# One pool of eight PSUM banks and a written-out order for every engine in a fused attention and feed-forward kernel

## The chip, the cores and the metric

The kernel runs on one core of one Trainium2 chip. The metric is the device time of one execution in microseconds. The kernel before was run three times: 359.77, 360.51 and 360.58 us, median 360.51 us.

## What is computed

The inputs are q, k and v, each (8, 8, 576, 64) in float32 (batch, heads, positions, head dimension), a bias table of 32 buckets by 8 heads, and the weights w_in (512, 2048) and w_out (2048, 512).

```python
scores = scale * np.matmul(q, k.transpose(0, 1, 3, 2))
...
scores = scores + bias.transpose(2, 0, 1)[None, :, :, :]
...
attn = np.exp(scores)
attn = attn / (np.sum(attn, axis=-1, keepdims=True) + 1e-09)
return np.matmul(attn, v).astype(np.float32)
```

The attention's result, 4608 rows of 512, goes through a feed-forward layer with a squared ReLU:

```python
h = np.maximum(x @ w_in, 0.0)
return (h * h @ w_out).astype(np.float32)
```

## The kernel before, in words

**Attention.** The 64 heads are worked on as 32 pairs (`pair`, L931; p = 4 * batch + hp). A pair's keys lie on TensorE's rows 0 to 63 for one head and 64 to 127 for the other, so that two score matmuls with 64 rows each run side by side (`scores_of`, L806: 128 keys by 512 queries, L815). The scores have the keys on the partitions. 576 keys are four key tiles of 128 and 64 last keys; 576 queries are 512 and 64 last queries, which have small matmuls of their own (L822). The 64 last keys of both heads share one matmul of 128 rows (`last_keys`, L1012). ScalarE takes the exponential from PSUM: 128 x 1024 elements at once over the two heads' banks (L997), 128 x 576 for the last keys (L1022), 128 x 256 per head for the last queries (`exp_of_last`, L831). VectorE multiplies the result by the table of exp(bias) (L728). `values` (L751) multiplies by v with a column of ones (L754, L761), and VectorE divides by the sum (L775, L780). The first batch goes in halves (`half_of_pair`, L840).

**Feed-forward.** The 4608 rows are nine groups of 512 (`layers`, L1483). The first product (L1501, or L1451 in halves for the first group) leaves 128 x 512 in a bank; ReLU takes it to SBUF (L1530, in this kernel always on ScalarE as `RELU_DVE` is 0), and VectorE squares it (L1540). Some units are done with seven products in place of eight (`by_sevens`, L1378). The second product also takes seven products in place of eight (`second`, L1204), combined by VectorE (L1232) or ScalarE (L1238), and SyncE stores the result.

**PSUM.** The eight banks are six tiles: two pairs of neighbouring banks (`sets_ps`, names st0 and st1, ring `r_set`) and four single banks (`g_ps`, names f0 to f3, ring `r_g`). Scores take a pair for each key tile, and two singles for the last queries.

**What sets the order.** The kernel's source first lists all work as operations (`Plan.add`), each with the engines that may do it, what it depends on and the buffers it uses. `Plan.schedule` then goes through them in planned time: each engine takes the operation that can start first, ties by due time; `DUES` gives due times for some 600 operations by their number. A buffer is taken from its ring when its first user starts, the one that has been free longest first (`min(ring.free)`). The instructions are then emitted in the order of planned starts, and each engine runs its own in that order. The waits between engines are not written in the source: the framework finds them from what each instruction reads and writes, in the order of emission.

In `pair`, batches from the second on compute two key tiles in one operation:

```python
            run([0, 1])
            last_keys()
            run([2, 3], True)
```

where `True` adds the last queries' eight matmuls to the operation, and their two exponentials after it. All of one operation's matmuls are issued one after the other.

Of the kernel before, what the change touches and what calls it, by code (L numbers as in the profile page):

```python
# [21 lines left out]
SCALE = 1.0 / 8.0  # L22
# [12 lines left out]
RELU_DVE = 0  # L35
# [31 lines left out]
DUES = """  # L67
# [52 lines left out]
"""  # L120
# [5 lines left out]
class Ring:  # L126


    def __init__(self, n, in_order=False):
        self.free = [(0.0, i) for i in range(n)]  # L130
        self.in_order, self.made, self.taken = in_order, 0, 0
# [39 lines left out]
STAY = 0.0  # L171


class Plan:
# [16 lines left out]
    def schedule(self):  # L191
        engines = ("PE", "ACT", "DVE", "POOL", "SP", "DMA", "XB")
        now = {"PE": 600.0, "ACT": 740.0, "DVE": 820.0, "POOL": 1300.0, "SP": 740.0, "DMA": 0.0, "XB": 0.0}
        mode = None
        waiting = {e: [] for e in engines}
        for op in self.ops:
            op.wait = len(op.deps)
            for d in op.deps:
                d.users.append(op)
            if not op.wait:  # L200
                for e in op.engs:
                    waiting[e].append(op)
        done = []
        while len(done) < len(self.ops):
            best = None
            for e in engines:
                pick = None
                for op in waiting[e]:
                    at = max(now[e], op.ready, self._buf_time(op))
                    if at == float("inf"):  # L210
                        continue
                    due = op.due if op.due > -1e8 else op.ready - 1e9
                    if e == "PE" and op.mode != mode:
                        due += STAY
                    key = (max(at, now[e]), due, op.seq)
                    if pick is None or key < pick[0]:
                        pick = (key, op)
                if pick is None:
# [9 lines left out]
            for x in op.engs:  # L228
                waiting[x].remove(op)
# [1379 lines left out]
```

## Time and profile before

| | |
|---|---|
| median of three runs | 360.51 us |
| profiled execution: first to last instruction (span) | 358.7 us |
| PE (TensorE matmuls) busy | 346.4 us, 97% |
| DVE (VectorE) busy | 297.5 us, 83% |
| ACT (ScalarE) busy | 272.6 us, 76% |
| POOL (GpSimd) busy | 170.6 us, 48% |
| matmuls | 4290 |

The page gives the profiled execution's span and not a time of its own beyond it; the median of the runs stands 1.8 us above the span. PE's busy time counts a matmul from its start to the moment its result has left the array, so neighbours overlap; what one matmul keeps the next from starting is read from the start times. In the views, a line such as L1204 is a line of the kernel; "x16" is the number of instructions merged in a row; square brackets hold idle time before a row and what ended it.

### The profile page before, as it was taken

The page shows a single profiled execution, that of the slowest core. Times are in us where ns is not written, and L with a number is a line of the kernel's source. Part 1 is how long each engine was busy: PE and PEld are TensorE (multiplying, and loading weights), DVE is VectorE, ACT ScalarE, POOL GpSimd, SP SyncE. Part 2 cuts the span into 40 slices and gives each one's busy share as a digit, 9 for nine tenths or more (in the row PEclk, how much of TensorE's full clock was granted, in tenths as well). Part 3 has the DMA queues.
Part 4 walks back from the last instruction along what each step waited for, and adds up shares of the span by engine and source line. Part 5 has one row for each costly group of instructions (what it writes and reads, how often), then busy time and mean ns, then how long its engine had stood idle before and what let it go on. Part 6 is the DMA issues. An engine that isn't in the chain of part 4 may idle for free.

```text
span 358.7 us, 10742 instructions
## 1 busy us (share of the span) xinstructions
PE 346.4 (97%) x4290; PEld 262.0 (73%) x4290; DVE 297.5 (83%) x673; ACT 272.6 (76%) x435; POOL 170.6 (48%) x289
## 2 busy tenths in 40 slices
PE   3988999999999999999999999999999999999996
PEld 3666788775587558877788568755867887888885
DVE  4888999666996799768896899798988798899993
ACT  4898997589966988678976887689889833899830
POOL 8886679698995896158478456221000000000000
PEclk9999999999999999999999999999999999999999
DMA  9999999999999999799999999863410032010023
GB/s 172 151 147 198 193 150 154 190 156 192 175 130 165 223 158 112 119 163 198 84 134 164 186 126 133 150 121 72 61 44 15 18 97 68 27 63 33 23 66 117
DMA packets 162210, 44.37 MB, mean 124 GB/s; under 512 B 145520, under 2 KB 162160, under 8 KB 162160
## 3 DMA queue, kind: packets, MB, share of 16 engines
q0 software_dynamic: 74208, 14.53, 54.6%
q1 hardware_dynamic: 87696, 28.86, 44.3%
q8 instruction: 33, 0.54, 0.6%
q10 hardware_dynamic: 256, 0.30, 0.3%
q14 instruction: 17, 0.14, 0.1%
HBM read 36.94 MB, written 9.44 MB: 129 GB/s over the span
## 4 chain that ended last, share of the span: by engine, by line
PE 88%; DMA 7%; POOL 2%; ACT 1%; issue 1%; DVE 0%; POOLq 0%
PE f L1204 31%; PE f L1501 20%; PE f L761 10%; PE st L815 8%; PE f L1378 7%; DMA w_in_sb<-in_moe_w_in_dram 5%; PE f L1451 3%; PE st L1378 3%; PE f L754 3%; PE st L1012 2%; DMA ks<-in_k_dram 2%; POOL va L368 2%; PE f L822 1%; PE f L1078 1%; POOL ks L368 0%
## 5 line engine op out<-in xcount | busy, mean ns | idle before, releaser
L997 ACT ACTIVATE pt<-st 128x1024 f16<-128x1024 f32 x112 | 111.1, 1031 | 23.0 <-PE st L815 22.8
L1501 PE MATMUL f<-xt,w_in_sb 128*128 128x512 f16 (+4 forms) x416 | 77.2, 330 | 0.0
L728 DVE TENSOR_TENSOR pt<-pt,tb_sb 128x512 f16<-128x512 f16 (+3 forms) x108 | 61.9, 581 | 12.6 <-ACT pt L997 9.3
L368 POOL DMA_DIRECT2D ks<-in_k_dram x79 | 55.9, 719 | 15.1 <-DMA kt<-ks 10.4
L1204 PEld LDWEIGHTS <-g 128*128 128x128 f16 x576 | 55.1, 98 | 7.6 <-issue 0.8
L368 POOL DMA_DIRECT2D qs<-in_q_dram x79 | 55.5, 712 | 8.1 <-DMA qt<-qs 6.2
L1530 ACT ACTIVATE rt<-f 128x512 f16<-128x512 f32 x80 | 47.3, 608 | 14.1 <-PE f L1501 12.7
L1501 PEld LDWEIGHTS <-w_in_sb 128*128 128x128 f16 x416 | 37.1, 98 | 26.7 <-issue 2.5
L761 PE MATMUL f<-va,pt 128*128 128x65 f16 x1280 | 53.2, 193 | 0.3 <-DMA va<-in_v_dram 0.3
L761 PEld LDWEIGHTS <-pt 128*128 128x128 f16 x1280 | 49.8, 97 | 1.3 <-issue 0.5
L1204 PEld LDWEIGHTS <-s 128*128 128x128 f16 x432 | 41.1, 98 | 5.8 <-issue 0.8
L1232 DVE SCALAR_TENSOR_TENSOR y<-f,y 128x512 f32<-128x512 f32 (+1 forms) x48 | 31.8, 665 | 12.5 <-PE f L1204 11.7
L815 PE MATMUL st<-qt,kt 64*128 64x512 f16 (+1 forms) x288 | 40.4, 361 | 1.0 <-DVE qt L716 0.6
L1540 DVE TENSOR_TENSOR g<-rt 128x512 f16<-128x512 f16 x80 | 34.3, 433 | 6.2 <-ACT rt L1530 5.3
L1204 PE MATMUL f<-wt,g 128*128 128x256 f16 x288 | 35.6, 273 | 0.0
L754 PE MATMUL f<-vm,pm 128*128 128x130 f16 x160 | 35.5, 222 | 0.0
L1204 PE MATMUL f<-w_out_sb,s 128*128 128x256 f16 x288 | 35.3, 273 | 0.0
L1204 PE MATMUL f<-w_out_sb,g 128*128 128x256 f16 x288 | 34.7, 273 | 0.1
L780 DVE TENSOR_TENSOR x<-f,r 128x384 f16<-128x384 f32 (+1 forms) x64 | 30.9, 485 | 0.9
L645 POOL CAST va<-f 128x512 f16<-128x512 f32 x24 | 16.7, 702 | 30.8 <-DMA f<-in_v_dram 17.5
L974 POOL COPY kz<-kt 64x64 f16<-64x64 f16 x55 | 19.4, 354 | 20.2 <-DMA kt<-ks 17.1
L831 ACT ACTIVATE pt<-f 128x256 f16<-128x256 f32 x64 | 22.9, 404 | 5.9 <-PE f L822 4.5
(112 smaller groups left out, 532.4 us busy)
## 6 DMA issues: line engine op xcount, KB each, us to landing
out_dram<-y SPq DMA_DIRECT2D x34, 256.0 KB, 2.8
f<-in_v_dram SPq DMA_DIRECT2D x24, 256.0 KB, 4.9
ks<-in_k_dram POOLq DMA_DIRECT2D x48, 64.0 KB, 5.2
qs<-in_q_dram POOLq DMA_DIRECT2D x48, 64.0 KB, 4.4
w_in_sb<-in_moe_w_in_dram POOLq DMA_DIRECT2D x4, 512.0 KB, 10.7
w_out_sb<-in_moe_w_out_dram POOLq DMA_DIRECT2D x4, 512.0 KB, 8.9
ks<-in_k_dram POOLq DMA_DIRECT2D x7, 144.0 KB, 5.6
qs<-in_q_dram POOLq DMA_DIRECT2D x7, 144.0 KB, 5.5
```

What stands on the lines that cost most here:

```text
L368: lambda: io(eng.dma_start(out=out_(), in_=in_())),
L728: io(nc.vector.tensor_tensor(out=a, in0=a, in1=t, op=MULT))
L754: nc.tensor.matmul(ps[:, i, :, :], pm[:, c : c + 128], vm[:, hp, :, 0:65], start=True, stop=False)
L761: nc.tensor.matmul(ps[:, i, e, :], pt[:, (2 * jt + e) * S + c : (2 * jt + e) * S + c + 128], va[:, jt, 2 * hp + e, 0:65], start=False, sto ...
L815: nc.tensor.matmul(banks[i][:, e, :], kt[rw[e], ts(jt, 128)], qt[rw[e], ds(q0, n)], start=True, stop=True)
L997: nc.scalar.activation(out=p5(pts[pb.slot])[:, jt, :, 0:512], in_=sets_ps[st.slot], func=EXPF, scale=SCALE)
L1204: nc.tensor.matmul(home[bf.slot][:, ts(s_, HALF)], left(c, s_), right(c), start=(c == 0 and (s_ == 0 or apart) and (own or i not in before ...
L1232: nc.vector.scalar_tensor_tensor(out=dst, in0=ps, scalar=OSC, in1=ys[y[plus].slot][:, cs], op0=MULT, op1=mybir.AluOpType.add,)
L1378: nc.tensor.matmul(ps()[:, ds(HALF * f + a, z - a)], left()[:, kk, ts(f, 128)], right(a, z)[:, kk, :], start=(first_ and f == 0 and a == 0 ...
L1501: nc.tensor.matmul(g_ps[bank.slot][:, a:z], w_in_sb[:, kk, ts(nt, 128)], xt_sb[:, kk, c : c + z - a], start=(kk == 0), stop=(kk == 3),)
L1530: io(nc.scalar.activation(out=rts[rb.slot], in_=g_ps[bank.slot], func=RELUF))
L1540: nc.vector.tensor_tensor(out=gs[gb1.slot][:, nt, :], in0=rts[rb.slot], in1=rts[rb.slot], op=MULT)
```

## The change

1. `TURNS` replaces `DUES`: five lists (PE, ACT, DVE, POOL, SP) name every operation by its number in the order in which that engine does it, 2112 in all. The list also fixes the engine where there was a choice. `Plan.schedule` still works out planned starts, for the order of emission and for which buffer of a ring is taken; at each step it takes the engine whose next entry can start first.
2. All eight banks are one tile and one ring. A pair of banks is any two that the ring gives; the exponential reads them with a stride (`in_two`).
3. Scores are one operation per key tile, and the last queries one of their own with one exponential of 128 x 512 for both heads.
4. ReLU may be done by VectorE (`RELU_DVE` is 9), squares by ScalarE.

The operations of a pair are numbered anew: from the second batch on a pair has twelve (score and exponential of key tiles 0 and 1, of the last keys, of key tiles 2 and 3, of the last queries) in place of ten.

```diff
-RELU_DVE = 0
+RELU_DVE = 9
-DUES = """
...
+TURNS = {
+    "PE": """
...
+1006 936 1033 1057 1059 1055 1101 1053 1102 1038 1051 1222 1049 1104 1105 1112 1116 1065 1070 1121 1125 1218
+1220 1250 1130 1134 1216 1248 1141 1212 1252 1254 1145 1142 1138 1152 1160 1153 1244 1246 1214 1156 1109 1085
...
+    "ACT": """
...
+927 1185 906 937 938 1060 1056 1054 1058 1223 1050 1052 1106 1219 1221 1251 1217 1249 1255 1213 1139 1143 1253
...
-    def schedule(self):
+    def schedule(self, order):
...
+        queues = {e: [self.ops[i] for i in l] for e, l in order.items()}
+        for e, l in queues.items():
+            for op in l:
+                op.engs = {e: op.engs[e]}
...
+            for e, l in queues.items():
+                if heads[e] == len(l) or l[heads[e]].wait:
                     continue
-                if best is None or pick[0][0] < best[0][0]:
-                    best = (pick[0], e, pick[1])
+                op = l[heads[e]]
+                at = max(now[e], op.ready, self._buf_time(op))
+                if at < (float("inf") if best is None else best[0]):
+                    best = (at, e, op)
...
-    sets_ps = [psum.tile([128, 2, 512], FP32, name=f"st{i}") for i in range(2)]
-    g_ps = pv_ps = [psum.tile([128, 512], FP32, name=f"f{i}") for i in range(4)]
+    banks_ps = psum.tile([128, 8, 512], FP32, name="bank")
+    g_ps = pv_ps = [banks_ps[:, i, :] for i in range(8)]
...
-    r_set, r_g, r_lane = Ring(2), Ring(4), Ring(8)
+    r_g, r_lane = Ring(8), Ring(8)
...
+    def squared(o, out_, src):
+        if o.eng == "ACT":
+            io(nc.scalar.activation(out=out_, in_=src, func=SQUAREF))
+        else:
+            io(nc.vector.tensor_tensor(out=out_, in0=src, in1=src, op=MULT))
...
+    def in_two(st):
+
+        i, j = st[0].slot, st[1].slot
+        return banks_ps[:, i : j + 1 : j - i, :] if i < j else banks_ps[:, j : i + 1 : i - j, :]
...
+    def last_queries(qb, pb, deps, T, after):
+
+        lq = [Buf(r_g) for _ in range(2)]
+        o = P.add(
+            {"PE": 4 * mm(64)}, lambda: scores_of(qb.slot, [], [], 0, 0, [of_head(lq, e) for e in range(2)]), deps,
+            [qb, pb] + lq, T, after, "r",
+        )
...
-        def run(jts, last=False):
-            sets = [Buf(r_set) for _ in jts]
-            lq = [Buf(r_g) for _ in range(2)] if last else []
+        def run(jt):
+            st = [Buf(r_g) for _ in range(2)]
...
+            def ex():
+                io(
+                    nc.scalar.activation(
+                        out=p5(pts[pb.slot])[:, jt, :, 0:512], in_=in_two(st), func=EXPF, scale=SCALE,
                     )
-
-                exps[jt] = P.add({"ACT": act(1024)}, ex, [o], [st, pb], T)
-            if last:
-                exps["q"], exps["q1"] = exp_of_last(lq, pb, o, T)
+                )
+
+            exps[jt] = P.add({"ACT": act(1024)}, ex, [o], st + [pb], T)
...
-        if b < 1:
-            run([0])
-            run([1])
-            last_keys()
-            run([2])
-            run([3], True)
-        else:
-            run([0, 1])
-            last_keys()
-            run([2, 3], True)
+        run(0)
+        run(1)
+        last_keys()
+        run(2)
+        run(3)
+        exps["q"] = last_queries(qb, pb, evac, T, after)
...
-    for op in P.schedule():
+    for op in P.schedule({e: [int(i) for i in x.split()] for e, x in TURNS.items()}):
```

The same replacement of `r_set` by the one ring is made in `last_keys`, in the halves of the first batch, and in `by_sevens`; the squares of both kinds of first product go through `squared`.

More of the change, by code (lines that the diff above doesn't have):

```diff
@@ L63, in _bucket @@
     return np.where(n < half, n, large).astype(np.int64)
-DUES = """
[52 rows of a table removed]
-"""
+TURNS = {
+    "PE": """
[26 rows of a table added]
+""",
+    "ACT": """
[17 rows of a table added]
+""",
+    "DVE": """
[29 rows of a table added]
+""",
+    "POOL": """
[11 rows of a table added]
+""",
+    "SP": """
[8 rows of a table added]
+""",
+}
 class Ring:
     def __init__(self, n, in_order=False):
-        self.free = [(0.0, i) for i in range(n)]
+        self.n, self.free = n, [(0.0, i) for i in range(n)]
         self.in_order, self.made, self.taken = in_order, 0, 0
@@ L170, in over @@
     return 40.0 if e == "POOL" else 0.0
-STAY = 0.0
 class Plan:
@@ L189, in land @@
         return op
-    def schedule(self):
-        engines = ("PE", "ACT", "DVE", "POOL", "SP", "DMA", "XB")
+    def schedule(self, order):
         now = {"PE": 600.0, "ACT": 740.0, "DVE": 820.0, "POOL": 1300.0, "SP": 740.0, "DMA": 0.0, "XB": 0.0}
         mode = None
-        waiting = {e: [] for e in engines}
+        queues = {e: [self.ops[i] for i in l] for e, l in order.items()}
+        for e, l in queues.items():
+            for op in l:
+                op.engs = {e: op.engs[e]}
+        moves = {e: [] for e in ("DMA", "XB")}
         for op in self.ops:
@@ L199, in schedule @@
                 d.users.append(op)
[L200 to L203, printed above, removed]
+            if not op.wait and op.fn is None:
+                moves[next(iter(op.engs))].append(op)
+        done, heads = [], dict.fromkeys(queues, 0)
         while len(done) < len(self.ops):
             best = None
[L206 to L218, printed above, removed]
-                    continue
-                if best is None or pick[0][0] < best[0][0]:
-                    best = (pick[0], e, pick[1])
+            for e, l in queues.items():
+                if heads[e] == len(l) or l[heads[e]].wait:
+                    continue
+                op = l[heads[e]]
+                at = max(now[e], op.ready, self._buf_time(op))
+                if at < (float("inf") if best is None else best[0]):
+                    best = (at, e, op)
+            for e, l in moves.items():
+                for op in l:
+                    at = max(now[e], op.ready)
+                    key = (at, op.due if op.due > -1e8 else op.ready - 1e9, op.seq)
+                    if best is None or at < best[0] or (best[1] == e and key < best[3]):
+                        best = (at, e, op, key)
             assert best is not None, "the plan is stuck"
-            (at, _, _), e, op = best
+            at, e, op = best[:3]
             took = op.engs[e]
@@ L227, in schedule @@
                 mode = op.mode
-            for x in op.engs:
-                waiting[x].remove(op)
+            if e in queues:
+                heads[e] += 1
+            else:
+                moves[e].remove(op)
             op.eng, op.start, op.end = e, at, at + took
@@ L247, in schedule @@
                     )
-                    for x in u.engs:
-                        waiting[x].append(u)
+                    if u.fn is None:
+                        moves[next(iter(u.engs))].append(u)
             done.append(op)
@@ L805, in values, with of_head @@
         return o
+    def in_two(st):
+        i, j = st[0].slot, st[1].slot
+        return banks_ps[:, i : j + 1 : j - i, :] if i < j else banks_ps[:, j : i + 1 : i - j, :]
+    def of_head(st, e):
+        i, j = st[0].slot, st[1].slot
+        return g_ps[(min(i, j), max(i, j))[e]]
     def scores_of(slot, banks, jts, q0, n, lq):
@@ L815, in scores_of @@
                     nc.tensor.matmul(
-                        banks[i][:, e, :], kt[rw[e], ts(jt, 128)], qt[rw[e], ds(q0, n)], start=True, stop=True
+                        banks[i][e], kt[rw[e], ts(jt, 128)], qt[rw[e], ds(q0, n)], start=True, stop=True
                     )
@@ L825, in scores_of @@
                 )
-    def exp_of_last(lq, pb, o, T):
-        def ex(e):
+    def last_queries(qb, pb, deps, T, after):
[5 more added lines that the diff above has]
+        def ex():
             io(
                 nc.scalar.activation(
-                    out=p5(pts[pb.slot])[:, :, e, 512:S],
-                    in_=g_ps[lq[e].slot][:, 0:256].rearrange("p (j s) -> p j s", j=4),
-                    func=EXPF, scale=SCALE,
+                    out=p5(pts[pb.slot])[:, :, :, 512:S].rearrange("p j e s -> p e j s"),
+                    in_=in_two(lq)[:, :, 0:256].rearrange("p e (j s) -> p e j s", j=4), func=EXPF, scale=SCALE,
                 )
             )
-        return [P.add({"ACT": act(256)}, lambda e=e: ex(e), [o], [lq[e], pb], T) for e in range(2)]
+        return P.add({"ACT": act(512)}, ex, [o], lq + [pb], T)
     def half_of_pair(p, part, turned):
@@ L851, in scores @@
         def scores(jt, last=False):
-            st = Buf(r_set)
-            lq = [Buf(r_g) for _ in range(2)] if last else []
+            st = [Buf(r_g) for _ in range(2)]
             def score():
-                banks = [sets_ps[st.slot][:, :, ts(j, 256)] for j in range(2)]
-                scores_of(qb.slot, banks, [jt, jt + 1], q0, 256, [g_ps[x.slot] for x in lq])
-            took = 2 * mm(256) + 10 + (4 * mm(64) if last else 0)
-            o = P.add({"PE": took}, score, evac + ready, [st, qb, pb] + lq, T, 0.0, "r")
+                banks = [[of_head(st, e)[:, ts(j, 256)] for e in range(2)] for j in range(2)]
+                scores_of(qb.slot, banks, [jt, jt + 1], q0, 256, None)
+            o = P.add({"PE": 2 * mm(256) + 6}, score, evac + ready, st + [qb, pb], T, 0.0, "r")
             def ex():
@@ L908, in half_of_pair @@
                 (512, lambda: tt(view(pb, 4 * S + 256, two + [[1, 256]]), tab(hp, 128, 256, 1)), [exps[2]] + tabs_done[2:6]),
-                (640, lambda: tt(view(pb, 6 * S + 256, two + [[1, 320]]), tab(hp, 0, 320, 1)), [exps[2], exps["q"], exps["q1"]] + tabs_done[0:5]),
+                (640, lambda: tt(view(pb, 6 * S + 256, two + [[1, 320]]), tab(hp, 0, 320, 1)), [exps[2], exps["q"]] + tabs_done[0:5]),
                 (192, lambda: tt(p4s[pb.slot][:, 384:S], tm_sb[:, hp, :]), [exps["k"]] + tm_done),
@@ L980, in pair, with ex @@
         exps = {}
-        def run(jts, last=False):
-            sets = [Buf(r_set) for _ in jts]
-            lq = [Buf(r_g) for _ in range(2)] if last else []
+        def run(jt):
+            st = [Buf(r_g) for _ in range(2)]
             def score():
-                scores_of(qb.slot, [sets_ps[st.slot] for st in sets], jts, 0, 512, [g_ps[x.slot] for x in lq])
-            took = len(jts) * mm(512) + 10 + (4 * mm(64) if last else 0)
-            o = P.add({"PE": took}, score, evac, sets + [qb, pb] + lq, T, after, "r")
+                scores_of(qb.slot, [[of_head(st, e) for e in range(2)]], [jt], 0, 512, None)
+            o = P.add({"PE": mm(512) + 3}, score, evac, st + [qb, pb], T, after, "r")
             if p == 4 * B - 1:
                 last_scores.append(o)
-            for jt, st in zip(jts, sets):
-                def ex(jt=jt, st=st):
-                    io(
-                        nc.scalar.activation(
-                            out=p5(pts[pb.slot])[:, jt, :, 0:512], in_=sets_ps[st.slot], func=EXPF, scale=SCALE
-                        )
-                    )
-                exps[jt] = P.add({"ACT": act(1024)}, ex, [o], [st, pb], T)
-            if last:
-                exps["q"], exps["q1"] = exp_of_last(lq, pb, o, T)
+            def ex():
+                io(
+                    nc.scalar.activation(
+                        out=p5(pts[pb.slot])[:, jt, :, 0:512], in_=in_two(st), func=EXPF, scale=SCALE
+                    )
+                )
+            exps[jt] = P.add({"ACT": act(1024)}, ex, [o], st + [pb], T)
         def last_keys():
-            st = Buf(r_set)
+            st = [Buf(r_g) for _ in range(2)]
             def score():
@@ L1012, in score @@
                         nc.tensor.matmul(
-                            sets_ps[st.slot][:, half, 0:HQ], kzs[qb.slot], qts[qb.slot][:, ts(half, HQ)],
+                            of_head(st, half)[:, 0:HQ], kzs[qb.slot], qts[qb.slot][:, ts(half, HQ)],
                             start=True, stop=True,
@@ L1016, in score @@
                     )
-            o = P.add({"PE": 2 * mm(HQ)}, score, evac + spread, [st, qb, pb], T, after, "f")
+            o = P.add({"PE": 2 * mm(HQ)}, score, evac + spread, st + [qb, pb], T, after, "f")
             def ex():
@@ L1023, in ex @@
                         out=p4s[pb.slot][:, 0:S].rearrange("p (h s) -> p h s", h=2),
-                        in_=sets_ps[st.slot][:, :, 0:HQ], func=EXPF, scale=SCALE,
+                        in_=in_two(st)[:, :, 0:HQ], func=EXPF, scale=SCALE,
                     )
                 )
-            exps["k"] = P.add({"ACT": act(S)}, ex, [o], [st, pb], T)
-        if b < 1:
-            run([0])
-            run([1])
-            last_keys()
-            run([2])
-            run([3], True)
-        else:
-            run([0, 1])
-            last_keys()
-            run([2, 3], True)
+            exps["k"] = P.add({"ACT": act(S)}, ex, [o], st + [pb], T)
+        run(0)
[4 more added lines that the diff above has]
+        exps["q"] = last_queries(qb, pb, evac, T, after)
         bands = [
@@ L1342, in by_sevens @@
                 late["ops", u] = late_sums(512, s_, terms, l_win + before, due + 10.0 * u, room)
-            home = r_set if g >= LATE else r_g
-            banks = {"a": Buf(home), "b": Buf(r_g), "c": Buf(r_g), "d": Buf(home)}
+            banks = {x: Buf(r_g) for x in "abcd"}
             y = {"u": Buf(r_f if g >= LATE else r_u), "v": Buf(r_y)}
@@ L1365, in by_sevens @@
                 st = banks[bk]
-                if bk in "ad" and g >= LATE:
-                    ps = lambda st=st: sets_ps[st.slot][:, 0, :]
-                else:
-                    ps = lambda st=st: g_ps[st.slot]
+                ps = lambda st=st: g_ps[st.slot]
                 parts = cut if i in (1, 2, 3) else [(0, HALF)]
@@ L1466, in by_halves, with square @@
                 r = one_of({"ACT": act(512), "DVE": dve(512)}, relu, [o], [bank, rb], 0.0)
-                def square(u=u, h=h, rb=rb):
-                    src = rts[rb.slot].rearrange("p (j s) -> p j s", j=2)
-                    io(
-                        nc.vector.tensor_tensor(
-                            out=gs[gb1.slot][:, 2 * u : 2 * u + 2, ts(h, HALF)], in0=src, in1=src, op=MULT
-                        )
+                def square(o, u=u, h=h, rb=rb):
+                    squared(
+                        o, gs[gb1.slot][:, 2 * u : 2 * u + 2, ts(h, HALF)],
+                        rts[rb.slot].rearrange("p (j s) -> p j s", j=2),
                     )
-                o = P.add({"DVE": dve(512, 2.0)}, square, [r], [rb, gb1], due - 1e5)
+                o = one_of({"DVE": dve(512, 2.0), "ACT": act(512)}, square, [r], [rb, gb1], due - 1e5)
                 for j in range(2):
@@ L1536, in layers @@
                 squares[g][nt].append(
-                    P.add(
-                        {"DVE": dve(512, 2.0)},
-                        lambda rb=rb, nt=nt, gb1=gb1: io(
-                            nc.vector.tensor_tensor(
-                                out=gs[gb1.slot][:, nt, :], in0=rts[rb.slot], in1=rts[rb.slot], op=MULT
-                            )
-                        ),
+                    one_of(
+                        {"DVE": dve(512, 2.0), "ACT": act(512)},
+                        lambda o, rb=rb, nt=nt, gb1=gb1: squared(o, gs[gb1.slot][:, nt, :], rts[rb.slot]),
                         [r], [rb, gb1], due - 1e5,
@@ L1571 @@
     layers(NG)
-    for x in DUES.split():
-        i, due = x.split(":")
-        P.ops[int(i)].due = float(due)
-    for op in P.schedule():
+    for op in P.schedule({e: [int(i) for i in x.split()] for e, x in TURNS.items()}):
         if op.fn is not None:
```

6 lines of the change are left out of this document (4 added, 2 removed), and 140 rows, old and new, of tables (DUES, TURNS).

## The prediction

> **What bounds the kernel now.** I read the page's busy shares first, then the busy time by stretches, then the waits of TensorE (PE), and last the start times of single matmuls.
>
> ```profile
> span 358.7 us, 10742 instructions
> ...
> PE 346.4 (97%) x4290; PEld 262.0 (73%) x4290; DVE 297.5 (83%) x673; ACT 272.6 (76%) x435; POOL 170.6 (48%) x289
> ```
>
> ```profile
> core 0: us, PE busy (x) PEld busy (x) DVE busy (x) ACT busy (x) POOL busy (x), PEclk, DMA share, GB/s
> 0.00:36.00 36.00, 26.91 (x526) 20.50 (x526) 26.84 (x83) 28.65 (x47) 28.28 (x54) 1.00 1.31 167
> 36.00:300.00 264.00, 263.90 (x3276) 193.53 (x3274) 222.35 (x508) 206.73 (x324) 142.30 (x235) 1.00 1.14 134
> 300.00:339.00 39.00, 39.00 (x344) 33.43 (x342) 34.99 (x63) 32.64 (x58) 0.00 (x0) 1.00 0.09 30
> 339.00:359.00 20.00, 16.55 (x152) 14.58 (x150) 13.27 (x23) 4.59 (x8) 0.00 (x0) 0.99 0.28 93
> ```
>
> From 36 us on PE never stands still until its last matmul: 263.90 of 264.00 and 39.00 of 39.00 us, at a granted clock of 1.00. Idle time is left in the first 36 us (9.1 us) and in the last 3 us. A busy PE need not be a fast one, so I look at when matmuls start.
>
> ```profile
> 128.63 0.38 PE L1501 MATMUL f<-xt,w_in_sb 128*128 128x512 f16 x1
> 128.84 0.60 PE L1378 MATMUL f<-tx,w_in_sb 128*128 128x256 f16 x4
> 129.28 1.89 PE L1501 MATMUL f<-xt,w_in_sb 128*128 128x512 f16 x8
> ```
>
> Columns: start, length, engine, line, tiles, weights, result, count. After one matmul of 512 columns the next starts 0.21 us later, after four of 256 the next one 0.44 us later (0.11 each). So each column costs about 0.42 ns, and the listed 0.38 us is 0.17 us longer than what keeps the next matmul waiting: the result leaves the array that much later. There is one more cost between neighbours:
>
> ```profile
> 35.65 0.60 PE L1451 MATMUL f<-xt,w_in_sb 128*128 128x256 f16 x4
> 36.18 0.60 PE L815 MATMUL st<-qt,kt 64*128 64x512 f16 x4
> 36.62 0.28 PE L822 MATMUL f<-qt,kt 64*128 64x64 f16 x8
> 36.83 0.23 PE L754 MATMUL f<-vm,pm 128*128 128x130 f16 x1
> ```
>
> Four full-height matmuls of 256 columns should let the next start after 0.44 us; the 64-row one starts after 0.53. Four 64-row matmuls side by side two by two take 0.44 us, as they should, and the eight of 64 columns should take 0.11 us where the next full-height one starts after 0.21. Each change between full height and half height costs about 0.10 us (over all of them 0.096). The timeline of PE has 154 changes of height or width of the array (transposes of 96 x 64 among them), the first at 4.41 to 6.24 us and the last at 287.45 to 287.99 us:
>
> ```profile
> 4.41 0.56 PE L419 MATMUL f<-g,id_sb 32*128 32x8 f32 x2 [4.41 <-DMA id_sb<-c_id]
> 6.24 0.69 PE L947 MATMUL f<-id_sb,ks 96*64 96x96 f16 x12 [1.27 <-ACT ex_sb L424]
> ...
> 287.45 0.61 PE L815 MATMUL st<-qt,kt 64*128 64x512 f16 x4
> 287.99 0.82 PE L1501 MATMUL f<-xt,w_in_sb 128*128 128x384 f16 x4
> ```
>
> So the kernel is a chain of matmuls at their full rate, plus 154 x 0.096 = 14.8 us of changes, plus the first 36 us. The change alters none of the matmuls. It can win only changes and idle time at the start, and anything that makes PE wait between 36 and 339 us is lost in full.
>
> **The change part by part.**
>
> *Changes of height.* I numbered the operations in the order in which the source lists them (a pair from the second batch on has two more than before) and marked the scores of 64 rows and the transposes in PE's table. Its 599 entries change 133 times, against 154: scores of different pairs and the last queries stand two or three together (23 visits of two entries, 37 of three, 3 of one). 21 x 0.096 = 2.0 us less. The Trainium skill (TensorEngine Tiling (Array Packing), section Tiling Modes) says that every change of tiling mode drains TensorE, which speaks against cutting the scores up by key tile; the trace agrees that a change costs, and the table's count decides how many there are.
>
> *The first 36 us.* The order of loads and first matmuls is another one, but each engine has the same kinds of work, and PE's longest waits there are for things that the tables do not remove:
>
> ```profile
> PE f L419 <- DMA id_sb<-c_id: 4.4, 1, 4.4
> PE f L1451 <- DMA w_in_sb<-in_moe_w_in_dram: 1.3, 1, 1.3
> PE f L947 <- ACT ex_sb L424: 1.3, 1, 1.3
> ```
>
> The load of w_in is the 22nd entry of POOL's table, about where it is now. I take 0, and 2 us either way, which is more than the wait for w_in.
>
> *ScalarE and VectorE.* By the tables 35 more ReLUs go to VectorE and 44 squares to ScalarE, and 64 exponentials of 256 become 32 of 512.
>
> ```profile
> L1530 ACT ACTIVATE rt<-f 128x512 f16<-128x512 f32 x80 | 47.3, 608 | 14.1 <-PE f L1501 12.7 <-ACT pm L1022 0.9
> L831 ACT ACTIVATE pt<-f 128x256 f16<-128x256 f32 x64 | 22.9, 404 | 5.9 <-PE f L822 4.5 <-issue 1.2
> L1424 ACT ACTIVATE g<-rt 128x512 f16<-128x512 f16 x32 | 20.0, 630 | 0.9
> L1540 DVE TENSOR_TENSOR g<-rt 128x512 f16<-128x512 f16 x80 | 34.3, 433 | 6.2 <-ACT rt L1530 5.3
> L1464 DVE TENSOR_SCALAR rt<-f 128x512 f16<-128x512 f32 x1 | 0.7, 682 | 0.0
> ```
>
> ScalarE: -35 x 0.608 + 44 x 0.630 - 64 x 0.404 + 32 x 0.608 = 0.0 us. VectorE: +35 x 0.682 - 44 x 0.433 = +4.8 us, to 302. Both stay far under PE's 346, which covers them; if that cover went they would still be 56 us short of being the bound. I take 0.
>
> *The one tile of eight banks.* This is the term that decides. The waits between engines come from the framework, which compares accesses within a tile. An access that strides over banks of a tile counts for it as the whole stretch from the first bank to the last: an exponential that reads banks 1 and 6 counts as touching 1 to 6. This is a property of the software, not of the chip, and before's trace cannot show it, since there a pair is a tile of two neighbouring banks. In the new kernel two things follow. An exponential also waits for products that were emitted ahead of it into banks in between, and a product emitted behind it into such a bank waits until the exponential has ended.
>
> How often do the pairs stand apart? The ring gives the bank that has been free longest. Following that rule down the five tables with the durations written in the source (used for which bank comes, never for a time of the kernel), I get two banks for each of the 188 activations over a pair (112 exponentials of key tiles, 28 of last keys, 32 of last queries, 16 of the first batch): only 51 pairs are neighbours; 40 are two apart, 25 three, 34 four, 16 five, 18 six, 4 seven. An example from the quoted rows of the tables: PE has 1218 1220 1250 1130 1134 1216, with banks 1 and 6; 0 and 4; 2 and 7; 3; 3; 1 and 6. The exponentials 1219, 1221 and 1251 are emitted behind 1220, 1130 and 1134. So 1219 (1 to 6) waits for 1220 (bank 4), and 1250 (bank 2) waits for 1219; 1221 (0 to 4) waits for 1130 (bank 3) and 1134 for 1221; 1251 (2 to 7) waits for 1134, and 1216 for 1251. PE and ScalarE, side by side today, take turns.
>
> What does one turn cost?
>
> ```profile
> L997 ACT ACTIVATE pt<-st 128x1024 f16<-128x1024 f32 x112 | 111.1, 1031 | 23.0 <-PE st L815 22.8
> ```
>
> ```profile
> 173.97 0.02 issue
> 173.99 0.57 ACT rt L1530
> ...
> 178.01 0.04 issue
> 178.06 1.03 PE f L1204 x8
> ```
>
> The last matmul's result 0.17 us after the next could have started, 0.02 to ScalarE's start, 1.03 for the exponential, 0.05 to PE's next start: 1.27 us (0.90 for the last keys at 0.661, 0.85 for the last queries at 0.61). For each of the 188 I took the last product ahead of it and the first behind it in its stretch, and added up PE's work in between at the rates above. In 41 cases there is none, in 38 others less than the turn needs; together 61.8 us are missing, 59.0 if places that overlap are counted once. What stands in ScalarE's queue between product and exponential (0.61 for an eviction, 1.03 for another exponential) lengthens turns: runs of up to six ScalarE entries, each place counted once, give 77 us, of which 9 come out as well when each access holds only its own banks; before's 263.90 of 264.00 us say that such runs cost little, so I take 77 - 9 = 68. Queued behind a waiting product is all of PE; ScalarE and VectorE wait for what it does not deliver, which leaves them slack.
>
> The ends: 40 us if the banks fall a third better than I followed them, since the order of planned starts decides that; 105 us if besides each of the 28 later pairs' last exponential comes a full turn (1.03) late for `values` (28 x 1.03 = 29), on top of the 77. Nearest to the rows is 68.
>
> Sum against the profiled execution: 358.7 - 2.0 + 0 + 0 + 68 = 424.7 us. The median of the runs stands 1.8 us above the span, so 426.5 us; with the ends and 2 us for the start, 396 to 466.
>
> **The rivals.**
>
> *The stretches do not bind.* If a strided access holds only its two banks, or the pairs fall side by side, nothing of the 68 us comes. Counted that way, the same places miss 0.5 us in all in place of 61.8: the order is comfortable by its own banks. Then 360.5 - 2.0 = 358.5 us, 356.5 to 360.5 with the start: faster. For it speaks the saturated PE, against it the 137 pairs that stand apart. It decides if fewer than about 2 of 79 short places really wait (2.0 us / 0.78 us each). Chance 0.11.
>
> *Every key tile is a visit of its own.* If the entries that stand together in PE's table did not run together, 28 x 3 = 84 visits more at two changes each cost 84 x 2 x 0.096 = 16 us: 376.6 us. PE runs its list in order, so this needs a slip in my numbering. Chance 0.02.
>
> *The clock falls.* With PE stopping every few us, the granted clock could drop. In the first 36 us PE is busy 26.91 of 36.00 us and the clock stays 1.00; the new middle would be busy 264 of about 330, more than that. If a quarter of PE's 346 us ran at half the clock, 87 us come on top: 513 us. The Trainium skill (TensorE: Matmul & The Clock Gate, section on HAM oscillation) describes kernels in which PE stands idle so often between groups of matmuls that the clock swings; by that rule this kernel is a candidate, by the row above it is not. Chance 0.02.
>
> **How the numbers follow.** The forecast, turns between PE and ScalarE, has 0.85, of which 0.05 outside 396 to 466 us. That range holds 0.80; the likeliest value is 426.5. It is about 18% slower than before. A measurement of this kernel tells apart about 0.3%, 1.1 us. Faster by more: 0.08, from the first rival; within: 0.03, the rest of it where the start eats the 2 us; slower: 0.89.
>
> **What would show it.** Right: PE's busy share falls from 97% to some 82%, with idle time in the stretch from 36 us on; among PE's waits there are dozens for the exponentials (key tiles, last keys, last queries) of about a microsecond, and ScalarE's exponentials wait for products that are not scores, such as those of the feed-forward layer. The clock is 1.00. Changes of height number 133. Busy times of VectorE near 302 and ScalarE near 273. Wrong: a PE that is still busy 264 of 264 us, or whose waits are for evictions or for `values` and not for exponentials.

## The result, and the profile after

The changed kernel takes 438.34 us (median of four executions, 432.41 to 438.99) against 360.50 us before (359.77 to 360.58). The ratio is 1.207, 95% interval 1.198 to 1.216; it is formed from the two executions that lie within 1.5% of the fastest, while the median is over all four (438.34 / 360.50 = 1.216).

From the page of the changed kernel: the span, the busy shares, and the granted clock in 40 slices of the span.

```profile
span 437.2 us, 10676 instructions
...
PE 364.6 (83%) x4290; PEld 267.5 (61%) x4290; DVE 303.8 (69%) x670; ACT 279.4 (64%) x408; POOL 165.6 (38%) x289
...
PEclk9959999999999999989999999999999999999999
```

TensorE has the same 4290 matmuls and is busy 83% of the span instead of 97%. The same view by stretches as before (busy time of each engine, then clock, DMA share and GB/s):

```profile
0.00:36.00 36.00, 25.01 (x393) 18.40 (x394) 20.34 (x58) 21.43 (x31) 22.06 (x42) 0.81 0.97 129
36.00:379.00 343.00, 284.84 (x3405) 201.03 (x3405) 235.68 (x530) 220.20 (x312) 143.54 (x248) 1.00 0.83 106
379.00:418.00 39.00, 39.00 (x351) 34.18 (x350) 34.71 (x60) 33.72 (x60) 0.00 (x0) 1.00 0.13 42
```

In the middle TensorE now stands still for 58.2 of 343.00 us; before it was 0.1 of 264.00. The 39 us that follow are as full as they were. Two things are new at the start: 393 matmuls are done by 36 us instead of 526, and the clock there is 0.81. What the idle time waits for stands in the waits of PE (us in total, times, longest):

```profile
PE bank L1553 <- ACT pt L1061: 9.7, 12, 1.1
PE bank L1262 <- ACT pt L1061: 9.5, 8, 1.6
PE bank L879 <- ACT pt L1061: 7.8, 8, 1.4
PE bank L1074 <- ACT pt L1061: 5.6, 6, 1.1
PE bank L809 <- ACT pt L1061: 5.3, 5, 1.6
PE bank L1432 <- ACT pt L1061: 3.7, 5, 1.1
```

L1061 is the exponential of a key tile. Added up over all rows of this kind, PE waits for exponentials of scores 68 times, 57.5 us. Before, there is one such wait:

```profile
PE st L815 <- ACT pt L864: 0.3, 1, 0.3
```

L1553, L1262 and L1432 are products of the feed-forward layer; they need no exponential's result. In the waits of all engines, exponentials in turn wait for such products, and VectorE waits for exponentials:

```profile
DVE y L1290 <- ACT pt L1061: 15.3, 2, 10.2
DVE rt L1584 <- ACT pt L1061: 11.9, 6, 3.4
ACT pt L1061 <- PE bank L1262: 10.3, 10, 1.5
ACT pt L1061 <- PE bank L1553: 7.3, 9, 1.4
ACT pt L1061 <- DVE y L1290: 5.5, 1, 5.5
```

The prediction's worked example can be found in the timeline of PE (start, length, operation; idle time before a row and its releaser in brackets):

```profile
134.55 0.60 PE L879 MATMUL bank<-qt,kt 64*128 64x512 f16 x4
136.52 0.39 PE L879 MATMUL bank<-qt,kt 64*128 64x512 f16 x2 [1.36 <-ACT pt L1061]
136.84 1.05 PE L1262 MATMUL bank<-wt,g 128*128 128x256 f16 x8
139.00 1.03 PE L1262 MATMUL bank<-wt,g 128*128 128x256 f16 x8 [1.11 <-ACT pt L1061]
139.87 0.29 PE L1074 MATMUL bank<-qt,kz 128*128 128x288 f16 x1
141.21 0.53 PE L1074 MATMUL bank<-qt,kz 128*128 128x288 f16 x3 [1.05 <-ACT pt L1061]
141.57 1.04 PE L1262 MATMUL bank<-w_out_sb,s 128*128 128x256 f16 x8
143.89 0.61 PE L879 MATMUL bank<-qt,kt 64*128 64x512 f16 x4 [1.28 <-ACT pm L1084]
```

and in that of ScalarE:

```profile
135.44 1.02 ACT L1061 ACTIVATE pt<-bank 128x1024 f16<-128x1024 f32 x1 [5.53 <-DVE y L1290]
137.93 1.02 ACT L1061 ACTIVATE pt<-bank 128x1024 f16<-128x1024 f32 x1 [1.46 <-PE bank L1262]
140.13 1.02 ACT L1061 ACTIVATE pt<-bank 128x1024 f16<-128x1024 f32 x1 [1.18 <-PE bank L1262]
142.65 1.19 ACT L1084 ACTIVATE pm<-bank 128x576 f16<-128x576 f32 x2 [1.49 <-PE bank L1262]
```

Read the two together. The products 1130 and 1134 (the two L1262 rows with `wt,g`) go to bank 3 and have nothing to do with scores. Yet the exponential at 137.93 starts when 1130 has ended, 1134 starts at 139.00 when that exponential has ended, the next exponential at 140.13 when 1134 has ended, and the rest of 1216 at 141.21 when that one has. PE and ScalarE take turns. The first exponential of the row adds something that the prediction did not have: its releaser is a VectorE read (L1290). The scores were there at 135.15 (134.55 + 0.60), so of the 5.53 us in the bracket the read made only the last 0.3.

### The profile page after: what moved, and what is told of

Read it like the earlier page. It is cut to its first block, busy times and chain, and to the rows that moved or that the text cites. A ratio compares the mean times of both kernels' runs of the same rounds, so it can differ in the third digit from the quotient of the medians.

```text
span 437.2 us, 10676 instructions
## 1 busy us (share of the span) xinstructions
PE 364.6 (83%) x4290; PEld 267.5 (61%) x4290; DVE 303.8 (69%) x670; ACT 279.4 (64%) x408; POOL 165.6 (38%) x289
## 4 chain that ended last, share of the span: by engine, by line
PE 66%; ACT 21%; DVE 6%; issue 3%; POOL 2%; DMA 2%; ACTq 0%; DVEq 0%; POOLq 0%
PE bank L1262 22%; ACT pt L1061 14%; PE bank L1553 13%; PE bank L1432 8%; PE bank L816 7%; PE bank L879 6%; PE bank L1505 3%; PE bank L809 2%; ACT pm L1084 2%; ACT pt L901 2%; DMA va<-in_v_dram 2%; PE bank L1074 2%; ACT pt L931 1%; DVE pt L783 1%; POOL va L417 1%
## 5 line engine op out<-in xcount | busy, mean ns | idle before, releaser
L1061 ACT ACTIVATE pt<-bank 128x1024 f16<-128x1024 f32 x112 | 111.5, 1022 | 51.8 <-PE bank L879 12.7
L1553 PE MATMUL bank<-xt,w_in_sb 128*128 128x512 f16 (+4 forms) x416 | 79.4, 330 | 10.7 <-ACT pt L1061 9.7
L1262 PEld LDWEIGHTS <-g 128*128 128x128 f16 x576 | 54.9, 98 | 22.1 <-issue 13.9
L1553 PEld LDWEIGHTS <-w_in_sb 128*128 128x128 f16 x416 | 36.9, 97 | 41.2 <-issue 19.1
L879 PE MATMUL bank<-qt,kt 64*128 64x512 f16 (+1 forms) x288 | 45.0, 377 | 14.4 <-ACT pt L1061 7.8
L816 PE MATMUL bank<-va,pt 128*128 128x65 f16 x1280 | 54.7, 194 | 0.6 <-DVE pt L783 0.5
L1290 DVE SCALAR_TENSOR_TENSOR y<-bank,y 128x512 f32<-128x512 f32 (+1 forms) x48 | 31.6, 663 | 31.2 <-ACT pt L1061 15.3
L1262 PEld LDWEIGHTS <-s 128*128 128x128 f16 x432 | 41.2, 98 | 10.7 <-issue 5.9
L809 PE MATMUL bank<-vm,pm 128*128 128x130 f16 x160 | 35.7, 223 | 7.5 <-ACT pt L1061 5.3
L1262 PE MATMUL bank<-wt,g 128*128 128x256 f16 x288 | 36.7, 277 | 5.9 <-ACT pt L1061 3.8
L1262 PE MATMUL bank<-w_out_sb,g 128*128 128x256 f16 x288 | 35.9, 273 | 4.3 <-ACT pt L1061 3.9
L1262 PE MATMUL bank<-w_out_sb,s 128*128 128x256 f16 x288 | 36.9, 274 | 2.6 <-ACT pt L1061 1.1
L835 DVE TENSOR_TENSOR x<-bank,r 128x384 f16<-128x384 f32 (+1 forms) x64 | 30.8, 485 | 9.2 <-ACT pt L1061 4.9
```

Source lines behind the costliest of these rows:

```text
L809: nc.tensor.matmul(ps[:, i, :, :], pm[:, c : c + 128], vm[:, hp, :, 0:65], start=True, stop=False)
L816: nc.tensor.matmul(ps[:, i, e, :], pt[:, (2 * jt + e) * S + c : (2 * jt + e) * S + c + 128], va[:, jt, 2 * hp + e, 0:65], start=False, sto ...
L835: nc.vector.tensor_tensor(out=xs[xb.slot][:, qt0 : qt0 + nq, :].rearrange("p t (e d) -> p t e d", e=2), in0=ps[:, :, :, 0:64], in1=rs[rb.s ...
L879: nc.tensor.matmul(banks[i][e], kt[rw[e], ts(jt, 128)], qt[rw[e], ds(q0, n)], start=True, stop=True)
L1061: nc.scalar.activation(out=p5(pts[pb.slot])[:, jt, :, 0:512], in_=in_two(st), func=EXPF, scale=SCALE)
L1262: nc.tensor.matmul(home[bf.slot][:, ts(s_, HALF)], left(c, s_), right(c), start=(c == 0 and (s_ == 0 or apart) and (own or i not in before ...
```

## The experiments

I state three theories. **Stretches:** the added waits come only from the stretch that a strided access counts for. **Order:** the new order, or finer operations, makes PE and ScalarE take turns with any banks. **One tile:** a single tile of eight banks costs something in itself, strided or not.

**Only the banks renamed.** The order, the operations, the shapes and the one tile stay. After the schedule has been made, each buffer gets its bank from a table, chosen so that no pair's stretch holds a bank that is in use beside it; most pairs become neighbours by it.

```diff
+BANKS = """
+1077610325414072306765672371422324560160152367601323454457016722353401064010235424074564651467572356
...
-    for op in P.schedule({e: [int(i) for i in x.split()] for e, x in TURNS.items()}):
+    order = P.schedule({e: [int(i) for i in x.split()] for e, x in TURNS.items()})
+    names = iter("".join(BANKS.split()))
+    named = set()
+    for op in P.ops:
+        for x in op.bufs:
+            if x.ring is r_g and id(x) not in named:
+                named.add(id(x))
+                x.slot = int(next(names))
+    for op in order:
```

> Tables, order of emission, instructions and their number are those of the changed kernel; only the bank numbers are given anew, so that no exponential's stretch holds a bank that is written or read beside it. Theory (waits through the stretch): the 78 us that PE stands longer go, 356 to 361 us, PE busy 97%, 133 changes of height (2 us less than before). Rival (the order of the tables, the smaller score operations or one ring cost the time by themselves): 430 us or more, as with the old numbers.

Measured: 359.85 us against 360.37 us for the kernel before on the same chip, ratio 0.9989 (0.9967 to 1.0011). The whole slowdown is gone. The timeline of PE for the same operations in this kernel:

```profile
106.83 0.82 PE L890 MATMUL bank<-qt,kt 64*128 64x512 f16 x6
107.58 1.92 PE L1273 MATMUL bank<-wt,g 128*128 128x256 f16 x16
109.34 0.65 PE L1085 MATMUL bank<-qt,kz 128*128 128x288 f16 x4
109.83 1.04 PE L1273 MATMUL bank<-w_out_sb,s 128*128 128x256 f16 x8
110.80 0.61 PE L890 MATMUL bank<-qt,kt 64*128 64x512 f16 x4
```

and ScalarE beside it:

```profile
107.29 2.85 ACT L1072 ACTIVATE pt<-bank 128x1024 f16<-128x1024 f32 x3 [4.48 <-PE bank L890]
```

From the first row to the last it is 3.97 us instead of 9.34; the three exponentials run one after the other while PE goes on. Since both kernels issue the same matmuls in the same order, their spans can be cut at the same matmul, number 393 and some 3400 later, where the last 59 us begin. First the changed kernel, then the one with renamed banks:

```profile
0.00:36.14 36.14, 25.01 (x393) 18.40 (x394) 20.35 (x59) 21.52 (x31) 22.20 (x42) 0.81 0.97 129
36.14:378.14 342.00, 283.98 (x3401) 200.64 (x3401) 235.22 (x529) 220.11 (x311) 143.40 (x248) 1.00 0.83 106
```

```profile
0.00:26.63 26.63, 19.95 (x393) 15.49 (x394) 19.32 (x57) 20.32 (x31) 19.69 (x36) 1.00 1.22 159
26.63:298.10 271.47, 270.62 (x3403) 197.95 (x3401) 233.43 (x529) 214.15 (x313) 151.85 (x254) 1.00 1.12 135
```

So of the 80.0 us between these two profiled executions 9.5 lie ahead of the 394th matmul, 70.5 in the some 3400 that follow, and none behind them. Order is ruled out as the cause, and so is One tile. That an exponential over distant banks is slow in itself is ruled out too: one of a key tile takes 1022 ns on average in the changed kernel and 1027 in this one.

**Two exponentials, each within one bank.** Banks and order of the changed kernel; every exponential over a pair becomes two instructions without a stride over banks (shown for key tiles; the other three kinds likewise).

```diff
-                io(
-                    nc.scalar.activation(
-                        out=p5(pts[pb.slot])[:, jt, :, 0:512], in_=in_two(st), func=EXPF, scale=SCALE
-                    )
-                )
+                for x in range(2):
+                    io(
+                        nc.scalar.activation(
+                            out=p5(pts[pb.slot])[:, jt, x, 0:512],
+                            in_=of_head(st, x), func=EXPF, scale=SCALE,
+                        )
+                    )
```

> Banks and order of the changed kernel; each exponential over two banks is two instructions, one for each bank, so that none strides. Theory: waits through the stretch go though the banks stay apart; ScalarE pays 156 x (2 x 0.608 - 1.03) = 29 us and some more for the last keys and queries, to about 312 us, under PE: 358 to 368 us. Rival (order or far banks as such): 430 us or more.

Measured: 361.44 us, ratio 1.0031 (1.0008 to 1.0053). The banks are as far apart as in the changed kernel, and PE is busy 347.2 us, 97% of the span, again. ScalarE has 188 instructions more and is busy 281.6 us, 9.4 us more than with renamed banks; my forecast of about 312 us was too high.

**Two exponentials, each over both banks.** The control: again two instructions, but each takes half the columns of both banks.

```diff
-                            out=p5(pts[pb.slot])[:, jt, x, 0:512],
-                            in_=of_head(st, x), func=EXPF, scale=SCALE,
+                            out=p5(pts[pb.slot])[:, jt, :, ts(x, 256)],
+                            in_=in_two(st)[:, :, ts(x, 256)], func=EXPF, scale=SCALE,
```

> As the kernel of one bank per instruction in the number of instructions, but each of the two still strides over both banks and takes half of the columns. Theory: the stretch stays, so the waits stay, 436 to 455 us. Rival (two short instructions in place of one long are what helps): as fast as the kernel of one bank per instruction.

Measured: 446.29 us, ratio 1.236 (1.230 to 1.242). With the same number of instructions as the run above, the stride alone makes 85 us. The first of PE's waits are those of the changed kernel again:

```profile
PE bank L1558 <- ACT pt L1064: 10.3, 11, 1.2
PE bank L1267 <- ACT pt L1064: 10.3, 9, 1.7
PE bank L879 <- ACT pt L1064: 8.3, 8, 1.4
```

**The kernel before, with one tile.** Its own order; the banks become one tile, pairs remain neighbours.

```diff
-    sets_ps = [psum.tile([128, 2, 512], FP32, name=f"st{i}") for i in range(2)]
-    g_ps = pv_ps = [psum.tile([128, 512], FP32, name=f"f{i}") for i in range(4)]
+    banks_ps = psum.tile([128, 8, 512], FP32, name="bank")
+    sets_ps = [banks_ps[:, 0:2, :], banks_ps[:, 2:4, :]]
+    g_ps = pv_ps = [banks_ps[:, i, :] for i in (4, 5, 6, 7)]
```

> The kernel before with all banks in one tile, its pairs still neighbours (0 and 1, 2 and 3). Theory (only the banks in between wait): no stretch holds another's bank, 360.4 us. Rival (one tile for all banks costs by itself): towards the 437.7 us that the same order took with pairs three banks apart.

Measured: 360.35 us against 359.79, ratio 1.0030 (0.9998 to 1.0062). One tile by itself costs at most 0.6%, and perhaps nothing.

**The kernel before, with its pairs apart.** The same one tile (`banks_ps`), with the two pairs as banks 0 and 3, and 4 and 7; the four single banks lie inside these stretches.

```diff
+    sets_ps = [banks_ps[:, 0:4:3, :], banks_ps[:, 4:8:3, :]]
+    g_ps = pv_ps = [banks_ps[:, i, :] for i in (1, 2, 5, 6)]
```

> The kernel before, its own order and its own due times; only the banks are one tile, the two pairs are banks 0 and 3 and 4 and 7, the singles 1, 2, 5, 6. Theory: 156 exponentials over a stretch with two singles in it, at 0.3 to 0.5 us each as worked out for such distances: 400 to 435 us, PE waiting for exponentials. Rival (the tables' order is what costs): 360.5 us, as nothing of the order is touched.

Measured: 437.73 us, ratio 1.215 (1.209 to 1.220), just above the interval that I gave. None of the change's order is in this kernel, and it is as slow as the changed one. Three rows of its waits: PE, VectorE and ScalarE, each waiting for work that it has no data from.

```profile
PE bank L1205 <- ACT pt L998: 17.9, 20, 1.2
DVE r L776 <- ACT pt L998: 21.1, 17, 2.3
ACT pt L998 <- PE bank L1205: 22.7, 16, 3.7
```

**How much by products, how much by reads.** The run before made VectorE's waits as large as PE's, and the prediction had counted only products. Three kernels rename the banks of the changed kernel as the first run does, with other tables. In two of them stretches hold banks that PE writes and none that VectorE or ScalarE reads, by the planned times. Counted as in the prediction, 37.0 and 99.2 us are missing (the changed kernel: 59.0). The third has hardly any such products (1.3 us) but stretches over banks that are being read out.

> As the one with 99 us, but with banks drawn at random and no readers in a stretch: 55 of 188 places short, 37.7 us missing, 37.0 with overlapping places once. If the time goes with that count: 359.9 + 37 = 397 us, up to 410 with ScalarE's queue. If instead a few stretches of the program bring all of the loss: near 360 or near 438.

Measured: 402.64 us, ratio 1.120 (1.116 to 1.124).

> Tables and order of the changed kernel, banks renamed so that stretches hold as many banks as possible in which PE writes beside the exponential, and none that VectorE reads beside it. The prediction's count: 123 of 188 places short of PE's work, 105.0 us missing, 99.2 with overlapping places once. Theory that the count is right in size: 359.9 + 99 = 459 us, up to 480 with ScalarE's queue. If VectorE's reads were a large part of what the changed kernel lost, less than that share: near 430.

Measured: 475.61 us, ratio 1.319 (1.311 to 1.326). One of its four executions took 685.25 us, at a mean granted clock of 0.55; the ratio leaves it out, and no run shows what made the clock fall so far. In the profiled execution, at a mean of 0.975, the clock fell in the middle as well:

```profile
290.00:310.00 20.00, 14.09 (x165) 10.06 (x162) 10.17 (x22) 8.00 (x11) 9.38 (x17) 0.74 0.68 77
```

> The other way round: stretches hold banks that VectorE reads beside the exponential (78 places in planned time, against 73 in the changed kernel) and hardly any that PE writes (10 places short, 1.3 us missing, against 79 and 59 us). Theory that only products count, as in the prediction: 360 to 362 us. Theory that readers wait for the stretch too, and give their banks back late: 365 to 385 us, VectorE waiting for exponentials in front of evictions.

Measured: 377.87 us, ratio 1.051 (1.048 to 1.054); that only products count, 360 to 362 us, is ruled out. The waits of this kernel show both directions, VectorE behind an exponential and an exponential behind VectorE:

```profile
DVE y L1301 <- ACT pt L1072: 7.2, 5, 2.5
...
ACT pm L1095 <- DVE x L846: 4.0, 1, 4.0
ACT pt L1072 <- DVE rt L1595: 3.4, 6, 1.2
...
DVE r L841 <- ACT pt L1072: 2.9, 4, 1.1
```

Added up over the rows of VectorE's reads of banks, they wait for exponentials of scores 31 times, 24.6 us, against once, 3.0 us, in the renamed kernel.

Above the renamed kernel's 359.85 us, products alone cost 42.8 us for 37.0 counted and 115.8 for 99.2: 1.16 and 1.17 us for each us of the prediction's count (the larger one at a mean clock of 0.975, which is in its figure). The renamed kernel was timed on another chip, on which the kernel before took 360.37 us and not 359.79; by ratios to these the rates come to 1.18 and 1.16. The kernel with reads costs 18.0 us, of which 1.3 are products by the count; PE itself still waits 13 times, 6.4 us, for exponentials there, so not all of it need be waits of reads. These reads only share a stretch with the exponential, and neither side writes what the other reads; the rows show them ordered all the same.

## Why the prediction was right, point by point

**The cause is shown.** Waits through the stretch make the slowdown: renaming banks takes it away (359.85), dropping the stride takes it away (361.44) while the same number of strided instructions keeps it (446.29), and a stretch over busy banks brings it to the kernel before (437.73).

**Its size: right, and some microseconds short.** The prediction had 68 us for products and the queue of ScalarE. By the rate of the two product kernels, the 59.0 us counted come to 59.0 x 1.16 = 68.5 us: the runs put 16% on top of the bare count where the prediction had put 15% for ScalarE's queue. That the two agree so well is partly luck, since the 15% was a difference of two counts (77 - 9) and no run separates the queue from the rest. The median of the changed kernel lies 438.34 - 359.85 = 78.5 us above the renamed one, which leaves 10 us that the sum did not have.

**Two things were left out: reads and the clock.** The prediction considered what PE writes into a stretch, and not what VectorE and ScalarE read from it. The kernel with reads, at 78 such places by its count, lost 18.0 us; the changed kernel has 73. The prediction also held the clock at 1.00. The one execution of the changed kernel at a clock of 0.996, which is also that of the kernel with 37.0 us counted, took 432.41 us; there 432.41 - 359.85 - 68.5 = 4.1 us are left for the reads. In the other three the clock was 0.98, and they took about 6 us more. How much the reads make beyond that cannot be separated: reads and products meet in the same places.

**The first 36 us: taken as 0, with 2 us either way.** For the order of loads and first matmuls alone, this was about right: in the renamed kernel PE is idle 6.7 us in the first 36, against 9.1 before, 2.4 us less. The changed kernel's first 393 matmuls come 9.5 us later than the renamed one's all the same. Stretches in the first batch are not new there, as its 16 exponentials were among the 188 counted; PE is idle 11.1 us ahead of that point instead of 6.7. The rest is that the same matmuls keep PE busy 25.01 us instead of 19.95, while the clock fell to half:

```profile
18.00:19.00 1.00, 0.61 (x11) 0.40 (x9) 0.99 (x3) 0.90 (x1) 0.96 (x3) 1.00 1.19 158
19.00:20.00 1.00, 0.27 (x1) 0.10 (x1) 0.32 (x2) 0.92 (x3) 1.00 (x3) 1.00 1.61 169
20.00:21.00 1.00, 0.44 (x13) 0.44 (x13) 0.46 (x3) 1.00 (x3) 0.47 (x1) 1.00 1.28 190
21.00:22.00 1.00, 1.00 (x24) 0.73 (x22) 0.97 (x5) 0.70 (x1) 0.00 (x0) 0.65 1.24 199
22.00:33.00 11.00, 9.17 (x99) 6.14 (x98) 6.00 (x18) 5.99 (x10) 1.48 (x4) 0.50 0.52 84
```

These are pieces of the changed kernel's span; PE is busy 1.32 us of the three from 18 to 21 us, and from 22 to 33 us it has half the clock. What sets the fall off is not shown: in its first 4 us PE was busy only 0.56 us, and the clock was 1.00 from there to 21 us. "The clock is 1.00" was therefore wrong at the start and right in the middle (1.00 from 36 us on).

**Of the rivals,** the first (stretches do not bind, 358.5 us) is refuted, and so is a separate visit for every key tile: PE's trace has 134 changes of height or width, the table's 133 and the one behind the first two matmuls of 32 rows. The 154 of before include that one, so 20 changes are saved and not 21, 1.9 us and not 2.0. The third, the clock, came true in small. Executions of the changed kernel at a mean clock of 0.98 took 437.73 to 438.99 us and one at 0.996 took 432.41: some 6 us, not 87. The Trainium skill (TensorE: Matmul & The Clock Gate, section A second HAM failure mode: psum-queue depth-cycling) describes a kernel whose clock swings because PE is idle briefly, but often, between groups of matmuls. In the changed kernel the trace bears this out only at the start: the middle, with PE idle 58.2 of 343.00 us in pieces of about a microsecond, kept 1.00. With still more waits it did not, as the kernel with 99.2 us counted shows (0.74 from 290 to 310 us, and 685.25 us in the execution at 0.55).

**The 2.0 us from fewer changes** did not show as a gain. The renamed kernel has the fewer changes and hardly any of the turns, and is faster by 0.4 us, with an interval from 1.2 faster to 0.4 slower, so a net gain of 2.0 us lies outside it. Its middle gives some of the gain back: PE idles 0.85 of 271.47 us there, where before it idled 0.10 of 264.00. PE's busy time, 346.2 us against 346.4, does not show the 2.0 us either, and why is open.

**ScalarE and VectorE** carry what was worked out: 272.2 and 301.6 us in the renamed kernel, against 273 and 302. In the changed one they show 279.4 and 303.8 and idle time throughout.

## What to carry to other kernels

The number of a PSUM bank is part of the schedule: where one instruction strides over banks of a tile, every bank between them is ordered with it, for those who write and those who read, so pairs must be neighbours, or in a tile of their own, or be read by an instruction for each bank. A pool with free pairing can keep its order and still be cured, by giving out the bank numbers after the order is fixed. In a trace, such waits show where an engine that used to be saturated is released by an instruction that has no data for it.

## What the runs showed of the hardware that was not expected

- Half the clock for more than 11 us after three microseconds in which PE was busy 1.32 us, while PE idle for a sixth of the 343 us in the middle kept all of it; and a mean clock of 0.55 over a whole execution of 685.25 us in the kernel with 99.2 us counted.
- Two exponentials in place of one cost ScalarE little. The groups of the key tiles' exponentials, in the changed kernel and in the one with an instruction for each bank, show total busy time and mean length of one:

```profile
L1061 ACT ACTIVATE pt<-bank 128x1024 f16<-128x1024 f32 x112 | 111.5, 1022 | 51.8 <-PE bank L879 12.7 <-PE bank L1262 10.3 <-PE bank L1553 7.3
```

```profile
L1064 ACT ACTIVATE pt<-bank 128x512 f16<-128x512 f32 x224 | 119.2, 637 | 14.4 <-PE bank L879 14.1
```

Twice 637 ns would be 1.27 us a pair, but the busy time is 119.2 / 112 = 1.06 us, since neighbours overlap; one wide exponential takes 1.00 by the same count.
